# Attention and two mixtures on one core: the second mixture unit by unit over all chunks, the first with batch 0 alone ahead

## The chip, the cores and the metric

The kernel runs on 1 core of one Trainium2 chip. The metric is the device time of one execution in microseconds (us); below, the median of several runs.

## The reference

Three stages follow each other. `x` is 4 batches x 8 heads x 512 tokens x 64, `state` the same with 32 tokens.

```python
scores = scale * x @ state^T;  a = softmax(scores);   xread = a @ state
scores2 = scale * state @ x^T; a2 = softmax(scores2); sread = a2 @ x
t = concat([xread, sread], axis=2)            # -> 2176 rows x 512
# first mixture, 512 -> 2048 -> 512
h = t @ w_in;  t = (h * tanh(softplus(h))) @ w_out
# second mixture, 512 -> 1536 -> 512
xn = t / rms(t) * rms_g
g = xn @ w_gate; v = xn @ w_val; out = (g * sigmoid(g) * v) @ w_out2
```

## The kernel before

All matmuls of the mixtures take each float32 operand as a high and a low float16 part and make three products. A **chunk** is a batch's 512 xread rows (chunks 0 to 3); the 128 sread rows of all batches are the small chunk 4. A **unit** is 512 hidden columns: 4 units in the first mixture, 3 in the second.

*Order.* Nothing runs in the order of the source. Each `op(...)` records an instruction, its engines, a guessed cost and its dependencies; `Plan` (L36) list-schedules them by latest start times and then writes the instructions out, so every engine's queue has a fixed order. `at` is an op's place on TensorE, `P.floor` a time before which an op is not urgent. A queue that waits holds up all that stands behind it on that engine.

*Weights of the first mixture* (`plain`, L628) are fetched through the buffers `stage` in `psm` (a pool in SBUF), turned from the raw words to float32 and split into parts, on VectorE (DVE: L575, L582, L591, L625) and ScalarE (ACT: L472, L580, L612). `pow2` (L481) makes a power-of-two scale per unit from ACT's sums of squares: a tiny matmul (L485) and five small DVE instructions.

*First mixture* (`group`, `l2`). Groups 0 to 5 take units as they come: unit 0 for batch 0, then for batch 1, unit 1 for both, units 2 and 3 for both. Each group ends with four evacuations that add to what the group before left in a slot (L1053). Group 6 is batch 2, group 7 the small chunk, group 8 batch 3, each with all four units. Folds (L944) make the weights of the first product, L988 applies it, L1036 is the second product.

*Weights of the second mixture* (`seven`, `keep`): each of the nine matrices (gate, value and out for three units) is made into eight blocks (Strassen-like sums, L675) in one of two regions of `psm` and `attm` and stored to DRAM in `kept` tensors. All nine are made while the first mixture runs. `conv` is the last of these conversions.

*Second mixture* (`gated`). For chunk after chunk: `rms` of the next chunk (a chain of DVE and ACT instructions, L1072 to L1137), then for each unit `gate` and `value` (`quad`: 7 products of 12 matmuls each, L1174, and the adds L1186), and the first three products of the output (`first_three`, L1258). The PSUM banks `a0` to `a2` collect all three units of a chunk. `finish` then runs the other four products over three units each and combines the banks with five adds (L1288) and two copies (L472). SBUF holds the weights of two units at most, so the weights of units are loaded again for every chunk (`load`, L1452). The eighth block of each matrix lives in the slots of chunks that are done (`load_rest`, L1464, L1470).

Of the kernel before, what the change touches and what calls it, by code (L numbers as in the profile page):

```python
# [32 lines left out]
class Op:  # L33
    __slots__ = (
        "engs", "fn", "deps", "succ", "bufs", "tab", "at", "due", "reserve", "lat", "name", "floor")


class Plan:
# [10 lines left out]
    @staticmethod  # L49
    def hop(a, b):  # L50

        return 0.0 if a == b else 0.7 if b == "T" else 0.2 if a == "T" else 0.14
# [17 lines left out]
    def op(self, engs, fn, r=(), w=(), tab=None, at=None, reserve=0, lat=0.0, after=(), due=None, name=""):  # L70
# [3 lines left out]
        o.succ, o.bufs = [], []  # L74
# [106 lines left out]
    def forward(self, late):  # L181
# [18 lines left out]
        while True:  # L200
            moved = True
            while moved:
                moved = False
                for e in free:
# [3 lines left out]
                    for o in waiting[e]:  # L208
# [5 lines left out]
                        key = late[o] + pen, self.index[o]  # L214
# [105 lines left out]
def attn_moe_moe_kernel(  # L320
# [69 lines left out]
    sxm, xem = Mem("sxm", 4), Mem("xem", 2)  # L390
# [9 lines left out]
    for n, m in enumerate((w1, attm, w1)):  # L400
        home["wg", n], home["wv", n] = (m, 0), (m, 3584)

    def spot(w, u, j):

        if j == 7:
            k = ("wg", "wv", "w2").index(w) + 3 * u
            return slotm[k // 4], k % 4 * 512
        if w == "w2":
            return (psm, 1536 * u + 512 * j) if j < 3 else (attm, 2048 * u + 512 * (j - 3))
        m, at = home[w, u]  # L410
        return m, at + 512 * j

    slots_xe = [
        [(sxm, 0), (sxm, 512), (xem, 0)],
        [(w1, 7168), (w1, 7680), (w2m, 7168)],
    ]
# [6 lines left out]
    P.fifo.update(("t", "g", "g2", "gb", "xb", "xt", "t2", "t3", "sbt", "m", "m3"))  # L423
    P.pool("t", [tt(512 * k, 512) for k in range(10)])
    P.pool("g", [gm(512 * k, 512, F16).rearrange("p (l f) -> p l f", l=2) for k in range(6)])
    P.pool("g2", [w2m(512 * k, 512, F16).rearrange("p (l f) -> p l f", l=2) for k in range(14)])
    P.pool("gb", [psm(4608 + 512 * k, 512, F16).rearrange("p (l f) -> p l f", l=2) for k in range(3)])
    P.pool("m", [rmsm(512 * k, 512, F16).rearrange("p (l f) -> p l f", l=2) for k in range(4)])
    P.pool("m3", [m(at, 512, F16).rearrange("p (l f) -> p l f", l=2)
                  for m, at in ((psm, 4608), (psm, 5120), (psm, 5632), (slotm[3], 1280))])  # L430
# [50 lines left out]
    def pow2(part, pnames, k, floor, nm, xexp, most=0, to=None):  # L481
# [4 lines left out]
           r=pnames, w=[b], reserve=0, name=f"pow2 {nm}")  # L486
# [52 lines left out]
    def fetch(w, u, dst, dn, pool="raw", after=()):  # L539
# [10 lines left out]
        for v in range(2):  # L550
# [8 lines left out]
            for j in range(2):  # L559
# [6 lines left out]
                last = op({"A": a_sb(512), "V": v2(512)}, hi, r=[r], w=dn(k), after=after, name=f"hi {w}{u}{k}")  # L566
# [18 lines left out]
                for part, fn, engs in (("s", sign, "V"), ("l", low, "AV")):  # L585
                    cost = {e: a_sb(512) if e == "A" else v2(512) for e in engs}
# [344 lines left out]

    m_users = {"m": [], "m3": []}

    def fold(c, u, pool, after):

        out = []
        for g in range(2):
# [635 lines left out]
```

## Time and profile before

| | |
|---|---|
| median of 3 runs | 808.26 us (807.59 to 808.39) |
| the profiled execution | 810.53 us; its span from first to last instruction 808.7 us |
| TensorE (PE) busy | 725.2 us, 90% of the span, mean granted clock 0.939 |
| weight loads (PEld) | 505.7 us, 63% |
| VectorE (DVE) busy | 645.5 us, 80%, 1237 instructions |
| ScalarE (ACT) busy | 451.6 us, 56% |
| HBM | 101.45 MB read, 23.33 MB written |

The matmul's end is modelled, so PE's busy time is not work at full rate; how much work PE does must be counted from its instructions. PEclk of 1.00 is 2.4 GHz, 0.50 is 1.2 GHz; a mean between them is a mixture of both.

### The profile page before, as it was taken

To read this page: it belongs to the slowest core of one execution; us is meant where nothing else is said; L and a number is where in the kernel's file an instruction comes from. 1 tells how busy PE (TensorE), PEld (TensorE's weight loads), DVE (VectorE), ACT (ScalarE), POOL (GpSimd) and SP (SyncE) were. 2 spreads that over 40 slices of the span, in tenths; PEclk is the share of its full clock that TensorE was granted. 3 is DMA by queue.
4 is the path that set the end of the run, shared out by engine and by line. 5 is a ranking of instruction groups with operands and counts; after the bars stand their busy time and mean duration, and the time that the engine had idled before them with its cause. 6 is when DMAs were issued, how large, how long until landed. Compare 5 with 4: busy or idle time off the path is not lost.

```text
span 808.7 us, 13823 instructions
## 1 busy us (share of the span) xinstructions
PE 725.2 (90%) x5606; PEld 505.7 (63%) x5606; DVE 645.5 (80%) x1237; ACT 451.6 (56%) x804; POOL 1.6 (0%) x7
## 2 busy tenths in 40 slices
PE   4465799999997989589999999999996999999997
PEld 3243344445443336373476788888885889989996
DVE  6999999859999998999635699479996878465771
ACT  7998987826969889947531255135563332111320
POOL 0000000000000000000000000000000000000000
PEclk8655999999998999888999999999999899999999
DMA  8977101106156566571752324375457435364101
GB/s 266 303 205 228 53 1 66 53 1 209 53 183 200 191 220 224 206 277 74 279 188 108 117 64 171 102 270 202 138 194 281 145 105 183 105 265 158 61 2 66
DMA packets 40772, 125.68 MB, mean 155 GB/s; under 512 B 20484, under 2 KB 20484, under 8 KB 35716
## 3 DMA queue, kind: packets, MB, share of 16 engines
q1 hardware_dynamic: 40708, 124.79, 44.2%
q8 instruction: 44, 0.72, 0.3%
q14 instruction: 20, 0.16, 0.1%
HBM read 101.45 MB, written 23.33 MB: 154 GB/s over the span
## 4 chain that ended last, share of the span: by engine, by line
PE 42%; DVE 14%; ACT 1%; DMA 1%; issue 1%; DVEq 0%; SPq 0%; ACTq 0%
PE p L1174 21%; PE a L1258 10%; PE a L1036 5%; PE p L988 3%; PE p L1334 2%; DVE tt L1186 2%; DVE tt L1236 1%; DMA out_dram<-slot 1%; PE a L1372 1%; DVE slot L1101 1%; DVE tt L1225 1%; DVE w2m L1217 1%; DVE rms L1128 1%; DVE attm L625 1%; DVE psm L625 1%
## 5 line engine op out<-in xcount | busy, mean ns | idle before, releaser
L1036 PE MATMUL a<-g,w2m 128*128 128x512 f16 (+1 forms) x960 | 191.9, 356 | 9.3 <-DVE g L1014 9.1
L1036 PEld LDWEIGHTS <-w2m 128*128 128x128 f16 x960 | 88.6, 102 | 99.7 <-issue 17.9
L1174 PEld LDWEIGHTS <-w 128*128 128x128 f16 x1344 | 132.0, 98 | 25.4 <-issue 7.6
L1186 DVE TENSOR_TENSOR tt<-p,tt 128x512 f32<-128x512 f32 x120 | 82.3, 686 | 47.8 <-PE p L1174 46.8
L1174 PE MATMUL p<-slot,w 128*128 128x256 f16 x768 | 93.3, 273 | 3.6 <-ACT tt L472 3.6
L1174 PEld LDWEIGHTS <-attm 128*128 128x128 f16 x672 | 66.0, 98 | 12.8 <-DMA attm<-kept_wg 2.8
L988 PE MATMUL p<-slot,rms 128*128 128x512 f16 x288 | 70.6, 389 | 3.3 <-ACT tt L1010 3.0
L1258 PE MATMUL a<-attm,w2m 128*128 128x256 f16 x576 | 65.3, 273 | 0.0
L1258 PEld LDWEIGHTS <-w2m 128*128 128x128 f16 x576 | 56.3, 98 | 6.5
L988 PEld LDWEIGHTS <-rms 128*128 128x128 f16 x288 | 28.3, 100 | 40.7 <-issue 10.7
L1010 ACT ACTIVATE tt<-p,page 128x512 f32<-128x512 f32 x68 | 45.2, 678 | 14.9 <-PE p L988 13.1
L1258 PE MATMUL a<-psm,g 128*128 128x256 f16 x432 | 51.9, 273 | 0.0
L1014 DVE SCALAR_TENSOR_TENSOR g<-tt,page,g 128x512 f16<-128x512 f32 x68 | 49.6, 746 | 1.7 <-ACT g L472 0.5
L472 ACT ACTIVATE w2m<-tt 128x512 f16<-128x512 f32 x43 | 25.7, 621 | 41.5 <-DVE tt L1225 30.0
L1174 PE MATMUL p<-slot,attm 128*128 128x256 f16 x384 | 46.0, 273 | 2.6 <-DMA attm<-kept_wg 2.6
L1210 ACT ACTIVATE tt<-tt,page 128x512 f32<-128x512 f32 x36 | 25.9, 721 | 38.3 <-DVE tt L1186 38.1
L1258 PEld LDWEIGHTS <-g 128*128 128x128 f16 x432 | 42.2, 98 | 5.3 <-DVE g L1217 0.3
L472 ACT ACTIVATE g<-tt 128x512 f16<-128x512 f32 x24 | 14.1, 621 | 51.1 <-DVE tt L1236 42.9
L472 ACT ACTIVATE g<-tt,page 128x512 f16<-128x512 f32 x39 | 27.1, 712 | 26.5 <-PE a L1036 26.5
L472 ACT ACTIVATE psm<-psm,page 128x512 f16<-128x512 f32 (+1 forms) x42 | 29.8, 715 | 9.3 <-DVE psm L625 7.3
L287 ACT ACT_TABLE_LOAD x27 | 34.6, 1283 | 0.5
L944 PE MATMUL p<-w,slot 128*64 128x512 f16 x192 | 26.9, 401 | 7.9 <-ACT tt L1010 4.4
(222 smaller groups left out, 1198.1 us busy)
## 6 DMA issues: line engine op xcount, KB each, us to landing
w<-kept_wg SPq DMA_DIRECT2D x8, 1792.0 KB, 7.2
w<-kept_wv SPq DMA_DIRECT2D x8, 1792.0 KB, 7.3
attm<-kept_w SPq DMA_DIRECT2D x12, 1024.0 KB, 5.1
psm<-in_moe_w_out_dram SPq DMA_DIRECT2D x10, 1024.0 KB, 5.9
psm<-in_moe_w_in_dram SPq DMA_DIRECT2D x8, 1024.0 KB, 5.5
attm<-kept_wg SPq DMA_DIRECT2D x4, 1792.0 KB, 9.5
attm<-kept_wv SPq DMA_DIRECT2D x4, 1792.0 KB, 9.0
psm<-in_moe_w_gate_dram SPq DMA_DIRECT2D x6, 1024.0 KB, 5.2
```

What stands on the lines that cost most here:

```text
L287: self.nc.scalar.preload_act_table_set(TABLES[table])
L472: nc.scalar.activation(o, i, ACTF.Copy, scale=1.0 if scale is None else scale)
L625: op({"V": v1(512)}, lambda e: nc.vector.scalar_tensor_tensor(lo, f, s, h, ALU.mult, ALU.subtract), r=[*fn_, *hn, sname], w=ln, name=f"sl ...
L944: nc.tensor.matmul(P[pm][64 * j:64 * j + 64, :], states(c)[:, g, j, a, :], part("wi", u, 2 * g + j, b), start=(a, b) == (0, 0), stop=(a, b ...
L988: nc.tensor.matmul(P[ph], P[folds[u][k]][:, a, f:f + 128], xh[:, k, b, :], start=(k, a, b) == (0, 0, 0), stop=(k, a, b) == (1, 1, 0))
L1010: op({"A": a_ps(512) + 0.09}, lambda e, s=s, ph=ph, ce=ce: nc.scalar.activation(P[s], P[ph], ACTF.Mish, scale=ce), r=[ph, cen], w=[s], tab ...
L1014: op({"V": v1(512) + 0.06}, lambda e, s=s, g=g, rh=rh: nc.vector.scalar_tensor_tensor(P[g][:, 1, :], P[s], rh, P[g][:, 0, :], ALU.mult, AL ...
L1036: nc.tensor.matmul(P[ya[d]][:, :n], part("wo", u, f, a)[:, d * 128:(d + 1) * 128], P[g][:, b, i * n:(i + 1) * n], start=first and m == 0, ...
L1174: nc.tensor.matmul(P[to][:, f * 256:f * 256 + 256], part(w, u, j, a)[:, k * 256 + f * 128:k * 256 + f * 128 + 128], h[:, k, b, :], start=b ...
L1186: op({"V": v1(512) + 0.06}, lambda e: nc.vector.tensor_tensor(P[to], P[bank_], P[a], ALU.add), r=[bank_, a], w=[to], name=f"{w} add")
L1210: op({"A": a_ps(512) + 0.09}, lambda e, i=i, o=o: nc.scalar.activation(P[o], P[i], ACTF.Silu, scale=c3), r=[i, f"c3{u}"], w=[o], tab="silu ...
L1258: nc.tensor.matmul(P[to][:, t * 256:t * 256 + 256], P[g][:, a, o:o + 128], part("w2", u, j, b)[:, f * 256:f * 256 + 256], start=begin and ...
```

## The change

The second mixture's loops change places: unit outside, chunks 0 to 3 inside. Each weight block is loaded once (nine reloads of 1.8 MB; `follow` puts the next matrix where one has had its last use). `finish` now runs for each unit and chunk, 12 times and over one unit. For the first two units its results go to DRAM as partial sums (four stores of 256 KB in each finish, the small chunk one); in the last unit both partial sums are read back, added (`parts`) and joined to the result (`more`). All `rms` are recorded ahead of the loop, and their parts and the eighth blocks get places of their own (`places`). Scales are per unit (`gated_scale`).

In the first mixture group 0, 1 and 2 are batch 0 (unit 0, unit 1, units 2 and 3); batch 1, 2, 3 and the small chunk follow whole. Six conversions are recorded early, three with the second mixture (`late_keeps`). The small matmul of `pow2` is put ahead of all else as soon as it is ready (`brief`) but leaves one bank free. Guessed costs in the planner change a little. All matmuls stay.

```diff
-                        key = late[o] + pen, self.index[o]
+                        key = -1.0 if o.brief else late[o] + pen, self.index[o]
...
-           r=pnames, w=[b], reserve=0, name=f"pow2 {nm}")
+           r=pnames, w=[b], reserve=1, brief=True, name=f"pow2 {nm}")
...
-            lprod(to, gs[nm], u, j, u == 0)
+            lprod(to, gs[nm], u, j, True)
...
-    def finish(c, gss, oa, between=()):
+    def finish(c, u, gs, oa, between=()):
+        last = u == U2 - 1
...
+        home_ = "o" if (u, c) > (0, 1) else "t"
...
+        if last:
+            for v in range(U2 - 1):
+                at = 2048 + 2048 * v
+                op({"D": 2.95}, lambda e, at=at, v=v: nc.sync.dma_start(out=psm(at, 2048), in_=parts[v, c][:, :]),
+                   r=[("part", v, c, k) for k in range(4)], w=psm.names(at, 2048), lat=1.9, name="part")
+            for i in range(2):
+                for j in range(2):
+                    a, b = 2048 + 512 * (2 * i + j), 4096 + 512 * (2 * i + j)
+                    op({"V": v1(512)}, lambda e, a=a, b=b: nc.vector.tensor_tensor(
+                        psm(a, 512), psm(a, 512), psm(b, 512), ALU.add),
...
         def over(to, nm, j):
-            for u in range(U2):
-                lprod(to, gss[u][nm], u, j)
+            lprod(to, gs[nm], u, j)
...
+        def more(a, i, j):
+            if last:
+                v, n = q[i, j]
+                op({"V": v1(512)}, lambda e: nc.vector.tensor_tensor(two(P[a]), two(P[a]), v, ALU.add),
+                   r=n, w=[a], name="end more")
...
+        def put(o, i, j):
+            if not last:
+                k = 2 * i + j
+                op({"D": 0.74}, lambda e: nc.sync.dma_start(out=parts[u, c][:, 512 * k:512 * k + 512], in_=P[o]),
+                   r=[o], w=[("part", u, c, k)], lat=1.9, name="part")
...
     def gated():
         before = None
-        for c in range(B):
-            if c + 1 < B:
-                rms(c + 1, slots_xe[(c + 1) % 2])
-            for u in range(U2):
...
+        rms(2, slots_xe[2])
+        rms(3, slots_xe[3])
+        rms(B)
+        for u in range(U2):
+            at = B - 1 if u < U2 - 1 else B - 2
+            for c in range(B):
+                oa = [buf(("oa", u, c, k), f"a{k}") for k in range(3)]
                 ss = gate(c, u)
...
+                if before is not None:
+                    v, d, gs, ob = before
+                    first_three(v, gs, ob)
+                    finish(d, v, gs, ob)
+                    if d == B - 1:
+                        small_end(v, small)
+                        follow("w2", v)
+                gs = value(c, u, ss)
...
+    def follow(w, u):
+        k = units.index(w) + 3 * u
+        for n in range(k + 1, 3 * U2):
+            if home[units[n % 3], n // 3] == home[w, u]:
+                waiting_loads.append((units[n % 3], n // 3))
+                break
+        ready_loads()
...
         group(0, 0, [0], None, 2)
-        group(1, 1, [0], None, 3)
-        group(2, 0, [1], 2, 2)
-        group(3, 1, [1], 3, 3)
-        group(4, 0, [2, 3], 2, 0)
+        group(1, 0, [1], 2, 2)
+        group(2, 0, [2, 3], 2, 0)
...
-        group(5, 1, [2, 3], 3, 1)
+        group(3, 1, every, None, 1)
...
+        late_keeps = {(0, 2): ("wg", 2), (1, 0): ("wv", 2), (1, 1): ("w2", 2)}
```

In the built programs DVE has 1317 instructions for 1237, ACT three table loads more, and PE the same matmuls. The three places below are on VectorE, which feeds PE and is fed by it. `psm` and `attm` hold weights on their way, `rms` working tiles of `rms`, `tt` results of the products, `a_`, `p_` PSUM banks, `slot_` the chunks, `page_` scales.

The first is at the end of the first mixture, where the small chunk's group needs its low part `g` (L1014, L1010 in the changed kernel). Before:

```order
L476 TENSOR_SCALAR psm<-psm,page_68 128x512
L625 SCALAR_TENSOR_TENSOR psm<-psm,page_68 128x512
L476 TENSOR_SCALAR attm<-attm,page_68 128x512
L625 SCALAR_TENSOR_TENSOR attm<-attm,page_68 128x512
L1014 SCALAR_TENSOR_TENSOR g<-tt,page_117,g 128x512 x2
```

Of the change:

```order
L1087 SCALAR_TENSOR_TENSOR rms<-rms 128x512
L587 SCALAR_TENSOR_TENSOR psm<-psm,sxm 128x2x256
L1089 TENSOR_TENSOR rms<-rms 128x512
L1010 SCALAR_TENSOR_TENSOR g<-tt,page_114,g 128x512
L1091 SCALAR_TENSOR_TENSOR rms<-rms 128x512
```

Two matrices in work at once stood ahead of that group; now it is one matrix and the `rms` of batch 1, which came a whole chunk later before.

The second is in the middle of the second mixture, where the eighth blocks are split (L1470, L1538 in the changed kernel). Before, near the end of chunk 1:

```order
L1137 TENSOR_TENSOR w2m<-rms,w2m 128x2x256
L1288 SCALAR_TENSOR_TENSOR slot_77<-a_88,page_117,tt 128x2x256
L1083 TENSOR_SCALAR rms<-p_83 128x128
L1091 SCALAR_TENSOR_TENSOR rms<-rms 128x128
L476 TENSOR_SCALAR slot_77<-tt,page_68 128x512
L1470 SCALAR_TENSOR_TENSOR slot_77<-tt,page_68,slot_77 128x512 x3
```

Of the change, in its first unit:

```order
L1223 TENSOR_TENSOR tt<-tt 128x512
L1538 SCALAR_TENSOR_TENSOR w2m<-tt,page_68,w2m 128x512
L1173 TENSOR_TENSOR tt<-p_84,tt 128x512
L1204 TENSOR_TENSOR w2m<-tt,w2m 128x512
L1173 TENSOR_TENSOR tt<-p_85,tt 128x512
```

The blocks went into `slot_77`, whose result had just been made and had to be stored first, and `rms` of the small chunk stood beside them; now they go into `w2m` between products' adds.

The third is the end of the program. Before:

```order
L1217 TENSOR_TENSOR w2m<-tt,w2m 128x512 x2
L1288 SCALAR_TENSOR_TENSOR tt<-a_88,page_117,tt 128x512
L1288 SCALAR_TENSOR_TENSOR slot_79<-a_89,page_117,tt 128x2x256 x2
L476 TENSOR_SCALAR slot_80<-a_90,page_117 128x512
L1288 SCALAR_TENSOR_TENSOR slot_79<-a_88,page_117,tt 128x2x256
```

Of the change:

```order
L1304 TENSOR_TENSOR rms<-rms,psm 128x512
L1411 TENSOR_TENSOR tt<-tt 128x512
L1298 SCALAR_TENSOR_TENSOR rms<-a_89,page_114,rms 128x512
L1436 SCALAR_TENSOR_TENSOR slot_81<-a_91,page_114,tt 128x512
L1304 TENSOR_TENSOR rms<-rms,psm 128x512 x2
L1298 SCALAR_TENSOR_TENSOR slot_80<-a_90,page_114,rms 128x2x256
L1298 SCALAR_TENSOR_TENSOR slot_80<-a_89,page_114,rms 128x2x256
L1298 SCALAR_TENSOR_TENSOR slot_80<-a_88,page_114,psm 128x2x256
```

The adds of the last chunk's finish gain the joining of the partial sums (L1304, L1411) between them.

## Rows read from the trace of the kernel before

**Rows 1.** The page, part 1: busy us, share of the span, instructions.

```profile
PE 725.2 (90%) x5606; PEld 505.7 (63%) x5606; DVE 645.5 (80%) x1237; ACT 451.6 (56%) x804; POOL 1.6 (0%) x7
```

**Rows 2.** Stretches: length, busy PE, PEld, DVE, ACT, POOL; PE clock, DMA share, GB/s.

```profile
0.00:100.00 100.00, 56.62 (x367) 33.64 (x368) 89.54 (x223) 90.20 (x170) 1.60 (x7) 0.71 0.70 213
100.00:160.00 60.00, 59.04 (x288) 26.06 (x287) 57.60 (x125) 49.08 (x86) 0.00 (x0) 1.00 0.12 40
160.00:188.00 28.00, 28.00 (x206) 13.73 (x206) 16.93 (x37) 9.11 (x17) 0.00 (x0) 1.00 0.13 29
188.00:240.00 52.00, 51.30 (x318) 23.99 (x314) 49.81 (x103) 42.20 (x79) 0.00 (x0) 1.00 0.40 137
240.00:375.00 135.00, 110.66 (x767) 60.83 (x766) 125.67 (x253) 114.37 (x222) 0.00 (x0) 0.87 0.60 217
375.00:540.00 165.00, 164.97 (x1247) 121.04 (x1244) 111.91 (x183) 60.48 (x96) 0.00 (x0) 1.00 0.40 146
540.00:600.00 60.00, 59.09 (x530) 51.80 (x528) 58.14 (x94) 33.07 (x50) 0.00 (x0) 1.00 0.52 190
600.00:640.00 40.00, 32.84 (x275) 27.84 (x274) 29.90 (x59) 15.03 (x28) 0.00 (x0) 0.91 0.58 213
640.00:808.00 168.00, 162.68 (x1627) 146.75 (x1624) 105.95 (x166) 38.02 (x62) 0.00 (x0) 1.00 0.34 124
```

**Rows 3.** Chain that ended last: start us, us, engine, what.

```profile
376.63 3.88 PE a L1036 x18
...
447.00 14.41 PE p L1174 x132
...
777.41 10.48 PE a L1258 x96
...
799.68 3.94 PE a L1258 x36
803.65 0.75 DVE slot L1288
```

**Rows 4.** The same chain between 333 and 347 us.

```profile
343.75 0.75 DVE attm L625
344.50 1.32 DVE g L1014 x2
```

**Rows 5.** Who waited for whom, PE, 240 to 375 us: total, times, longest.

```profile
PE a L1036 <- DVE g L1014: 9.1, 2, 8.3
PE p L485 <- ACT junk L612: 4.2, 2, 2.1
```

**Rows 6.** The same, DVE, 100 to 200 us.

```profile
DVE g L476 <- PE a L1036: 7.0, 2, 5.1
DVE slot L1053 <- PE a L1036: 4.4, 4, 2.3
```

**Rows 7.** The same, all engines, 600 to 640 us.

```profile
ACT slot L472 <- DMA out_dram<-slot: 3.9, 1, 3.9
...
DVE slot L476 <- DMA out_dram<-slot: 3.6, 1, 3.6
...
PE p L1174 <- ACT tt L472: 2.9, 1, 2.9
...
PE p L1174 <- DMA attm<-kept_wg: 2.6, 1, 2.6
```

**Rows 8.** Groups of DVE instructions: busy us, mean ns | idle before.

```profile
L1186 DVE TENSOR_TENSOR tt<-p,tt 128x512 f32<-128x512 f32 x120 | 82.3, 686 | 47.8 <-PE p L1174 46.8
...
L1236 DVE TENSOR_TENSOR tt<-tt 128x512 f32<-128x512 f32 x48 | 32.4, 685 | 0.6
...
L1288 DVE SCALAR_TENSOR_TENSOR slot<-a,page,tt 128x512 f32<-128x512 f32 x12 | 9.0, 748 | 10.2 <-PE a L1258 10.1
```

**Rows 9.** DMA issues: count, KB each, median us to landing.

```profile
w<-kept_wg SPq DMA_DIRECT2D x8, 1792.0 KB, 7.2
...
tt<-kept_wg SPq DMA_DIRECT2D x3, 256.0 KB, 5.1
```

More of the change, by code (lines that the diff above doesn't have):

```diff
@@ L958, in fold, with group @@
         return out
[L960 removed]
+    def group(gi, c, us, before, after):
         n = width[c]
@@ L1301, in finish @@
+        if last:
+            c11, c12, c21, c22 = ((lambda v=v: v, n) for v, n in (place(0, 0), place(0, 1), place(1, 0), place(1, 1)))
+        else:
+            c11, c12, c21, c22 = ((t(o), [o]) for o in (x11, u2, a1, u3))
+        op({"A": a_ps(512) + 0.13, "V": v1(512) + 0.06}, lambda e: copy_to(e, two(P[a1]), two(P[A]), osc),
+           r=[A, on_], w=[a1], after=opened[1:] if home_ == "o" else (), name="end copy")
+        add(t(u2), [u2], B_, t(a1), [a1])
+        more(u2, 0, 1)
         over(B_, "S3", T3)
-        add(lambda: two(P[u3]), [u3], B_, a1)
+        add(t(u3), [u3], B_, t(a1), [a1])
@@ L1303, in finish @@
+        more(u3, 1, 1)
+        more(a1, 1, 0)
         over(A, "A12", W21)
-        scaled(lambda: c11[0], c11[1], A)
-        add(lambda: c22[0], c22[1], C, u3)
+        if last:
+            add(*c11, A, lambda: q[0, 0][0], q[0, 0][1])
+        else:
+            scaled(*c11, A)
+            put(x11, 0, 0)
+        add(*c22, C, t(u3), [u3])
+        put(u3, 1, 1)
         over(C, "S4", W22)
-        add(lambda: c12[0], c12[1], C, u2)
+        add(*c12, C, t(u2), [u2])
+        put(u2, 0, 1)
@@ L1310, in finish @@
         over(B_, "A22", T4)
-        add(lambda: c21[0], c21[1], B_, a1)
+        add(*c21, B_, t(a1), [a1])
+        put(a1, 1, 0)
+        if not last:
+            return
         for i in range(2) if c == B - 1 else [None]:
@@ L1426, in gated @@
-        finish(B - 1, *before, [lambda: small_end(small_gs)])
+                if c == B - 1 and u < U2 - 1:
+                    follow("wg", u)
+                if before is not None:
[6 more added lines that the diff above has]
+                gs = value(c, u, ss)
+                if c == at:
+                    small = small_value(u, sb_)
@@ L1429, in attn_moe_moe_kernel, with keep @@
+                if c == B - 1 and u < U2 - 1:
+                    follow("wv", u)
+                before = u, c, gs, oa
+                if (u, c) in late_keeps:
+                    later_keep(*late_keeps[u, c])
+                if c == B - 2 and u < U2 - 1 or c == 0 and u == U2 - 1:
+                    load_rest(u)
+        u, c, gs, ob = before
+        first_three(u, gs, ob)
+        finish(c, u, gs, ob, [lambda: small_end(u, small)])
     kept = {}
-    def keep(w, u, k, after):
+    def keep(w, u, k, floor, after=()):
```

298 lines of the change are left out of this document (145 added, 153 removed).

## The prediction

> **What bounds the kernel now.** I read the page's busy times first [rows 1]. PE is busy 90% of the span and DVE 80%. As PE's ends are modelled, I counted its work by matmuls instead. A 512-column matmul runs at 3.88/18 = 0.216 us and a 256-column one at 14.41/132 = 0.109 us, both at the full clock [rows 3]. All matmuls of the mixtures come to 647 us at these rates, and I estimate 38 us for attention, transposes and the small ones: 685 us of PE work. The change adds no matmul, so the span can only move by what stands beside these 685 us, which is 808.7 - 685 = 124 us.
>
> Where these lie shows in the stretches [rows 2]. I call the time less the PE work done until then PE's **lag**, counting the matmuls in each stretch at the rates above. The lag is 70 us at 100 us (fetching, conversion and attention, with the clock at 0.71), still 68 at 188, 105 at 375, 105 at 540, 107 at 600, 117 at 640 and 119 at the end; a tail of 5 us follows. So there are three places: the start, the stretch from 188 to 375 (37 us), and 540 to 660 (14 us).
>
> From 240 to 375 PE is busy 110.7 of 135 us at a mean clock of 0.87, while DVE is busy 125.7 of 135 [rows 2]: DVE is the bound there. The wait that ends last is on DVE's `g`, 9.1 us, 8.3 of it in one piece [rows 5], and in the chain that `g` stands right behind the splitting of weights in `attm` and `psm` [rows 4]. Just before, from 160 to 188, DVE was busy only 16.9 of 28 us and PE all of it [rows 2]; DVE waited 7.0 + 4.4 us for products [rows 6], having nothing else to do in its order. The late loss has another cause. From 600 to 640, ACT and DVE wait 3.9 and 3.6 us to write into a slot that is still being stored, PE then waits 2.9 us for a copy that stands behind this on ACT, and 2.6 us for a reloaded gate matrix [rows 7].
>
> **The change, part by part.** *DVE's work.* Counted in the built orders, five adds in each of 12 finishes instead of 4, one more in each of the last four, and the small chunk's, are 45 more scalar-tensor-tensor adds, at 748 ns [rows 8]. Joining the partial sums adds 29 plain adds at 685 ns [rows 8]. That is 33.7 + 19.9 = 53.5 us by rows, or 49 us as busy time (DVE's rows overlap: they sum to 703 us for 645.5 busy). Eight evacuations of the first mixture go, and 13 more copies are shared between ACT and DVE. Cover: from 375 us on DVE is busy 111.9 + 58.1 + 29.9 + 106.0 = 306 of 433 us [rows 2], so 127 us are idle; ACT has more. Without that cover the adds would cost 53.5 us.
>
> *The order.* What counts is how much DVE work stands ahead of a given matmul. For matmuls with the same PE work ahead of them, I summed the DVE instructions ahead of what they wait for, scaled to the page's busy time, and subtracted the PE work. This lead is the least lag that the order allows:
>
> | PE work ahead | 30 | 120 | 180 | 270 | 390 | 525 |
> |---|---|---|---|---|---|---|
> | lead before | 61 | 47 | 52 | 70 | 34 | 18 |
> | lead after | 59 | 54 | 55 | 47 | 59 | 29 |
>
> At 270 us of PE work 728 DVE instructions are needed before and 687 after. The hump at 270 goes, because batch 1 and batch 3 fill PE while the matrices are converted, and a lower one, from the `rms` of all chunks and the last conversions, comes at 390. (The three late conversions are not late in the built order: two end ahead of the second mixture's products, the third with its first chunks. The table has that in it.) Only this hump, 59 against 70, is a gain that the order guarantees.
>
> To the lead comes the time that DVE loses. Before, the lag at 375 us was 105 for a lead of 70: 35 us, which is DVE's idle time until then (375 - 339.6 busy) [rows 2]. After, I keep the 10 us of the first 100 us. Over the next 380 us, with DVE needed almost all the time, I bound the loss by the two nearest rows: 2.4 of 60 us (100 to 160), and 11.5 of 187 us (188 to 375) [rows 2], so 15 to 23 us. The 11 us of 160 to 188 need not come back, since the order leaves DVE no such lull (lead 54 and 55 for 47 and 52). The lag at 390 us of work is then 59 + 10 + 15 to 23 = 84 to 92; I take 88, in the middle, because each stretch mixes both kinds. Before it was 104.5 there. **Term 1: -16 us**; its ends are -27 (lag 77, where PE's own 70 is near) and -5.
>
> *The late loss.* The reloads for each chunk go (the gate's into `w` alone are 8 of 1.8 MB, 7.2 us each [rows 9]), no block is put into a slot being stored, and no `rms` stands there. DVE is fuller than before, as it was from 540 to 600: 58.1 of 60 us, while PE lost 0.9 us of idle time [rows 2]. Scaled to 265 us that makes 4 us for 14. **Term 2: -10 us**; ends -13 and 0.
>
> *Stores.* Each early finish stores four times 256 KB; a 256 KB load lands in 5.1 us [rows 9]. The four buffers in `rms` must be free at the next finish, 27.5 us of PE work later (two quads of 84 and one output of 84 matmuls at 0.109 us). I cost this at nothing; without the cover, at most 5 us for each of eight finishes, 40 us. The SP queue keeps its order, so a load that waits for a matrix's last use holds stores behind it; the only such places are the matrix changes, and no load stands there with less than a chunk to go.
>
> *The end.* In the last finish each product has 12 matmuls, 1.31 us, where 36 covered DVE's add for 3.94 us [rows 3]. Four adds of 0.75 us [rows 3] and three joins of 0.69 may show. From 0 to 5 us; I take the lower half, as the small chunk's product stands between. **Term 3: +2 us.**
>
> The sum is -16 - 10 + 2 = -24 us. The profiled execution took 810.53 us, 2.3 above the median of 808.26, so I expect 810.5 - 24 - 2.3 = **784 us**, with 776 to 796 where each term goes half-way to its ends.
>
> **The rivals.** *PE alone decides* (chance 0.11). If DVE stays ahead throughout, the lag stays near 72 in the plateau: -32, late -11, end +1, so 766 us. For it: from 100 to 188 PE lost nothing [rows 2]. Against: both engines are needed all the time, and each small wait of one is passed on.
>
> *The front keeps its losses* (0.16). DVE's losses move with it, waiting for raw weights, ACT's squares or banks; the wait for squares is 4.2 us from 240 to 375 [rows 5]. With 42 us of loss at 390 the lag is 101: -4, late -6, end +2: 800 us, up to no change.
>
> *Handoffs make it slower* (0.08). In each finish PE's next product on a bank waits for DVE to have read it. Before, three units stood between (3.94 us), now one (1.31 us). If one add of 0.75 us shows at each of 4 handoffs in 12 finishes, that is 36 us: 820 us. It decides from 24 us on, half a us for each handoff. For it: DVE will be busy about 355 of 410 us there. Against: from 540 to 600 DVE was 97% busy and PE lost 0.9 us [rows 2], and DVE's adds wait for PE 46.8 us in all [rows 8], seldom the reverse; the order puts other products' adds between a finish's adds. The Trainium skill (Perfetto Trace Analysis, Identifying the Most-Contended Engine) says that the engine with the highest occupancy is the one to relieve, and that for VectorE occupancy is a fair measure, while TensorE's headroom is to be read from its weight loads. By that rule DVE (80% against 63%) is the contended engine and loading it with 49 us more makes about 857 us. The trace does not bear it out for the second mixture: from 640 on DVE idles 62 of 168 us and PE is busy 162.7.
>
> *The clock* (0.04). Many short waits of PE could bring a mean clock of 0.91 to the second mixture, as from 600 to 640 [rows 2]: 9% of some 390 us, 35 us, 819 us. From 540 to 600, with short waits too, it stayed at 1.00. The Trainium skill (TensorE: Matmul & The Clock Gate, A second HAM failure mode: psum-queue depth-cycling) describes a kernel whose frequent micro-idles between groups made the clock swing between its levels; by it the shorter finishes speak for this rival.
>
> **How the numbers follow.** The forecast has 0.61. A measurement tells about 0.2%, 1.6 us. Faster are the forecast, PE alone, and most of the second rival (0.13): 0.85. No change is 0.04: the upper end of that rival (0.03) and 0.01 of the last two; the rest of those makes slower 0.11. The range is 766 to 803: below it lies half of the first rival, above it the last two and the upper part of the second.
>
> **What would show it.** Right: DVE busy near 694 us; from 240 to 375 us PE waits on DVE's `g` gone and the clock above 0.95; a lag near 88 where the second mixture's first unit ends; no wait on `out_dram` or on a reloaded matrix; PE without gaps over 1 us from there to the last finish. Wrong: DVE idle more than 30 us between 100 and 480, waits of PE on the end adds in every finish, or waits of DVE on stores of partial sums.

## The result and the profile after

The changed kernel takes **772.31 us** (median of 4 runs, 771.34 to 773.05); beside it on the same chip the kernel before takes 808.33 us. The ratio is 0.9555, with an interval of 0.9539 to 0.9572. The forecast was 784 us in a range of 766 to 803: sign and range held, and the gain is 12 us larger than forecast. The profiled execution took 771.34 us, its span 769.6 us (before 810.53 and 808.7 us).

The page's busy times, which answer to [rows 1]:

```profile
PE 705.1 (92%) x5606; PEld 494.4 (64%) x5606; DVE 683.2 (89%) x1317; ACT 454.2 (59%) x808; POOL 1.6 (0%) x7
```

DVE is busy 37.7 us more than before, and the span is 39.1 us shorter. The stretches that answer to [rows 2] (length, then busy time and count of PE, PEld, DVE, ACT, POOL; PE's clock, DMA share, GB/s):

```profile
0.00:100.00 100.00, 53.58 (x337) 29.07 (x338) 90.79 (x224) 92.19 (x167) 1.59 (x7) 0.73 0.70 213
100.00:160.00 60.00, 60.00 (x399) 28.33 (x398) 56.64 (x137) 56.40 (x102) 0.00 (x0) 1.00 0.22 67
160.00:188.00 28.00, 28.00 (x144) 12.60 (x144) 26.44 (x56) 24.00 (x38) 0.00 (x0) 1.00 0.26 95
188.00:240.00 52.00, 50.51 (x318) 23.15 (x314) 48.94 (x104) 40.71 (x81) 0.00 (x0) 1.00 0.48 172
240.00:375.00 135.00, 134.28 (x751) 64.84 (x750) 128.28 (x253) 101.61 (x198) 0.00 (x0) 1.00 0.53 189
375.00:540.00 165.00, 158.45 (x1560) 138.34 (x1559) 143.17 (x249) 78.75 (x129) 0.00 (x0) 1.00 0.24 85
540.00:600.00 60.00, 60.00 (x554) 53.80 (x553) 52.31 (x85) 18.67 (x30) 0.00 (x0) 1.00 0.25 85
600.00:640.00 40.00, 40.00 (x415) 36.39 (x413) 29.81 (x48) 12.32 (x19) 0.00 (x0) 1.00 0.45 159
```

From 240 to 375 us PE goes from 110.66 busy at a clock of 0.87 to 134.28 at 1.00, and from 600 to 640 us from 32.84 to 40.00. Of the waits of PE from 240 to 375 us [rows 5] only one is left:

```profile
PE p L1077 <- DVE rms L1072: 0.7, 1, 0.7
```

The lag, counted as in the prediction, answers to its terms:

| PE work done, us | 30 | 120 | 240 | 270 | 330 | 390 | 420 | 525 | 660 | tail after it |
|---|---|---|---|---|---|---|---|---|---|---|
| lag before | 70.5 | 67.6 | 85.1 | 104.8 | 103.6 | 104.4 | 104.6 | 117.3 | 118.7 | 5.4 |
| lag after | 67.7 | 67.8 | 62.7 | 62.8 | 68.8 | 73.7 | 75.1 | 75.2 | 75.1 | 9.9 |

**Term 1** (lag at 390) is -30.7 us, forecast -16. **Term 2** (from there to the end: 1.4 us instead of 14.3) is -12.9, forecast -10. **Term 3** (tail) is +4.5, forecast +2. The sum is -39.1 us, the difference of the spans. The 38 us of PE work for attention and the small matmuls are an estimate. So the entries up to 240 are rough: with these matmuls priced by their columns at one rate they move by up to 10 us, those of both kernels from 270 on by 2 at most. The fall of the lag between 120 and 240 lies within that.

### The profile page after: what moved, and what is told of

Read it like the earlier page. It is cut to its first block, busy times and chain, and to the rows that moved or that the text cites. A ratio compares the mean times of both kernels' runs of the same rounds, so it can differ in the third digit from the quotient of the medians.

```text
span 769.6 us, 13980 instructions
## 1 busy us (share of the span) xinstructions
PE 705.1 (92%) x5606; PEld 494.4 (64%) x5606; DVE 683.2 (89%) x1317; ACT 454.2 (59%) x808; POOL 1.6 (0%) x7
## 3 DMA queue, kind: packets, MB, share of 16 engines
HBM read 67.90 MB, written 32.24 MB: 130 GB/s over the span
## 4 chain that ended last, share of the span: by engine, by line
PE 47%; DVE 33%; ACT 12%; DMA 4%; issue 3%; SPq 0%; POOL 0%; POOLq 0%; ACTq 0%; DVEq 0%
PE p L1161 22%; PE a L1245 11%; PE a L1032 5%; PE p L984 4%; DVE psm L621 3%; DVE g L1010 3%; DVE tt L1173 2%; PE p L1372 2%; ACT sxm L576 2%; ACT junk L608 2%; DVE psm L472 2%; ACT w2m L468 2%; DVE attm L621 1%; ACT w L468 1%; DVE rms L1124 1%
## 5 line engine op out<-in xcount | busy, mean ns | idle before, releaser
L1161 PEld LDWEIGHTS <-attm 128*128 128x128 f16 x1008 | 98.4, 98 | 16.9 <-issue 5.6
L1161 PEld LDWEIGHTS <-w 128*128 128x128 f16 x1008 | 98.6, 98 | 11.3
L1173 DVE TENSOR_TENSOR tt<-p,tt 128x512 f32<-128x512 f32 x120 | 82.1, 684 | 21.6 <-PE p L1161 21.0
L984 PE MATMUL p<-slot,rms 128*128 128x512 f16 x384 | 90.8, 383 | 3.0 <-ACT tt L1006 3.0
L1161 PE MATMUL p<-slot,attm 128*128 128x256 f16 x576 | 69.7, 273 | 3.3 <-DVE tt L470 1.6
L1161 PE MATMUL p<-slot,w 128*128 128x256 f16 x576 | 69.3, 273 | 0.0
L1010 DVE SCALAR_TENSOR_TENSOR g<-tt,page,g 128x512 f16<-128x512 f32 x68 | 49.1, 744 | 0.6 <-ACT g L468 0.5
L1245 PE MATMUL a<-attm,w2m 128*128 128x256 f16 x384 | 46.7, 273 | 2.3 <-DVE rms L1298 1.3
L576 ACT ACTIVATE sxm<-psm 128x512 uint16<-128x512 uint16 x49 | 37.0, 779 | 10.7 <-DMA psm<-in_moe_w_out_dram 6.7
L621 DVE SCALAR_TENSOR_TENSOR psm<-psm,page 128x512 f16<-128x512 f32 x49 | 36.6, 746 | 1.5 <-ACT psm L468 0.8
L1298 DVE SCALAR_TENSOR_TENSOR rms<-a,page,rms 128x512 f32<-128x512 f32 x38 | 28.3, 745 | 7.7 <-PE a L1245 7.6
L1245 PE MATMUL a<-attm,g 128*128 128x256 f16 x288 | 34.7, 273 | 0.0
```

The lines of the kernel that those rows point to most:

```text
L576: nc.scalar.activation(s16[:, :, 0], r16[:, :, 1], ACTF.Copy, scale=2.0 ** -13, bias=2.0 ** -14 - 0.5)
L621: op({"V": v1(512) + 0.06}, lambda e: nc.vector.scalar_tensor_tensor(lo, f, s, h, ALU.mult, ALU.subtract), r=[*fn_, *hn, sname], w=ln, nam ...
L984: nc.tensor.matmul(P[ph], P[folds[u][k]][:, a, f:f + 128], xh[:, k, b, :], start=(k, a, b) == (0, 0, 0), stop=(k, a, b) == (1, 1, 0))
L1010: op({"V": v1(512) + 0.06}, lambda e, s=s, g=g, rh=rh: nc.vector.scalar_tensor_tensor(P[g][:, 1, :], P[s], rh, P[g][:, 0, :], ALU.mult, AL ...
L1161: nc.tensor.matmul(P[to][:, f * 256:f * 256 + 256], part(w, u, j, a)[:, k * 256 + f * 128:k * 256 + f * 128 + 128], h[:, k, b, :], start=b ...
L1173: op({"V": v1(512)}, lambda e: nc.vector.tensor_tensor(P[to], P[bank_], P[a], ALU.add), r=[bank_, a], w=[to], name=f"{w} add")
```

## Experiments

Each edit goes through the planner again, so the order of the whole program moves with it. The lag tells where a difference arose. All ratios are to the kernel before on the same chip.

### Which side of the change brings the plateau

The first four runs put one side of the change back or carry it over alone. Theory A gave term 1 to the first mixture (groups, powers, cost guesses), theory B to the second mixture's new order.

`b_groups`, the kernel before with the new groups:

```diff
-        attention(1)
...
+        attention(1)
...
-        group(1, 1, [0], None, 3)
-        group(2, 0, [1], 2, 2)
-        group(3, 1, [1], 3, 3)
-        group(4, 0, [2, 3], 2, 0)
+        group(1, 0, [1], 2, 2)
+        group(2, 0, [2, 3], 2, 0)
...
-        group(5, 1, [2, 3], 3, 1)
+        group(3, 1, every, None, 1)
```

> The kernel before, with the changed kernel's order of the first mixture alone (batch 0 alone on the first conversions, then batch 1, then batches 2 and 3; the second attention recorded after all plain tails). Theory A, the first mixture's order holds the 31 us that term 1 turned out to be worth: in its built order the DVE work needed ahead of PE's 270th us of work still leads by 65 us (70 before, 47 in the changed kernel), so by the lead alone 5 us go, but if the waits for conversions and powers go with the old order, 20 to 30 us go: 780 to 790 us, and the lag at 390 us of PE work is 75 to 85. Theory B, the gain sits in when the second mixture's matrices are converted against the first mixture's products: 800 to 808 us, lag at 390 about 100, with the wait of over 5 us on the gates g near 345 us still there.

Measured: 796.25 us, ratio 0.9835 (0.9819 to 0.9852), lag 92.2 at 390 us of PE work: between the theories.

`b_both` adds the powers:

```diff
-                        key = late[o] + pen, self.index[o]
+                        key = -1.0 if o.brief else late[o] + pen, self.index[o]
...
-           r=pnames, w=[b], reserve=0, name=f"pow2 {nm}")
+           r=pnames, w=[b], reserve=1, brief=True, name=f"pow2 {nm}")
```

> The kernel before, with the new order of the first mixture and the new handling of the powers (put first when ready, with one of the two spare accumulators' bank held back). Theory A: as the run with the groups alone or up to 5 us faster, 775 to 788 us, the PE gaps before the powers (8.6 us between 100 and 375 us in the kernel before) gone. Theory B: 800 to 808 us, lead 63 at 270 us of PE work and a lag there above 95.

Measured: 792.62 us, 0.9793 (0.9778 to 0.9809), lag 86.5: between again. Its stretch from 240 to 375 us:

```profile
240.00:375.00 135.00, 125.28 (x892) 67.28 (x891) 128.88 (x252) 107.56 (x205) 0.00 (x0) 0.99 0.53 194
```

PE gains 14.6 us of busy time there over [rows 2], with as much DVE work.

`a_groups`, the changed kernel with the old groups (the diff of `b_groups` backwards):

> The changed kernel with the old order of the first mixture (batches 0 and 1 in turn on the first conversions, the second attention early). Theory A: the plateau's gain is lost, 795 to 803 us, lag at 390 us of PE work about 100. Theory B: the second mixture's new order keeps it, 770 to 776 us; its lead is 39 to 50 between 240 and 390 us of PE work (47 to 59 in the changed kernel), so the lag stays at 68 to 76.

Measured: 773.81 us, 0.9559 (0.9544 to 0.9573), lag 71.7: theory B. In the changed kernel the order of the groups is worth nothing measurable.

`a_pow2`, the changed kernel with the old powers (`reserve=0`, no `brief`):

> The changed kernel with the powers as before (no bank held back, no priority). Theory A, with the powers as its part: gaps of PE before the powers come back, 5 to 10 us, 777 to 782 us. Theory B: 769 to 774 us. In its built order DVE has far less to do ahead of PE between 210 and 330 us of PE work (lead 20 to -2 against 46 to 53) and again 34 at 390; so if the lead, and not PE's own floor near 68 us, set the plateau, the lag would fall to 55 or less there and the time to 760 us or less. I expect the floor to hold: a lag does not fall unless PE's work stands idle behind nothing, and PE cannot make up time once lost.

Measured: 791.74 us, 0.9774 (0.9755 to 0.9794): slower than both allowed, and not by gaps before the powers. The lag was lower than in the changed kernel (57.1 at 240 us of PE work, below the 68 that I had taken for a floor; the entries are rough there) and then jumped from 61.0 to 88.1 between 330 and 345. PE's waits from 375 to 440 us:

```profile
PE p L1161 <- DMA attm<-kept_wg: 21.3, 1, 21.3
```

That is the reload of the second mixture's first gate matrix. SP's timeline (start, length, line) shows why it is late:

```profile
351.32 0.32 SPq L1500 DMA_DIRECT2D w<-kept_w  x1
393.42 0.32 SPq L1489 DMA_DIRECT2D kept_wv<-psm  x1
402.64 0.32 SPq L1489 DMA_DIRECT2D kept_wv<-psm  x1
403.05 0.38 SPq L1500 DMA_DIRECT2D attm<-kept_wg  x1
```

It stands in SP's queue behind stores of blocks that DVE had not split yet, and goes out at 403.05 us as soon as the last of them has gone; in the changed kernel it goes out at 311.6. Without priority, four of the second mixture's powers had been made by 312 us, where the changed kernel had made eight. So here, as far as this one run tells, the priority keeps the stores, and with them the queue, moving. It is no source of term 1: with other groups and guesses the old powers do no harm (`a_second`, below).

The next pair carries over the whole first mixture, or all but it. `b_first` is `b_both` with the new cost guesses too; `a_second` is the changed kernel with the old groups, the old powers and the old guesses (such as these):

```diff
-        return 0.09 if a == b and a in 'VA' else 0.0 if a == b else 0.7 if b == "T" else 0.2 if a == "T" else 0.14
+        return 0.0 if a == b else 0.7 if b == "T" else 0.2 if a == "T" else 0.14
...
-            op({"A": a_sb(size) + 0.07}, fn, r=ns, w=[q, (nm, "n", i)], lat=SLACK, name=f"sq {who}")
+            op({"A": a_sb(size) + 0.17}, fn, r=ns, w=[q, (nm, "n", i)], name=f"sq {who}")
```

> The kernel before with everything the change does to the first mixture: the order of the groups, the handling of the powers, and the planner's new cost guesses. The second mixture is the old one. Theory A, the first mixture's order holds term 1: 778 to 785 us, lag at 390 us of PE work 74 to 80, and only the late loss (14 us) left of the difference. Theory C, formed on the four runs before this one (the same 31 us are reached from either side, because what costs is DVE standing without work while a power of two is outstanding, and each part only shortens such a stop): the guesses give at most 5 us on top of the 792.6 us of groups and powers together: 787 to 793 us. Its built order leads by 68 us at 270 us of PE work, so a lag under 80 there would speak against lead plus idle time of DVE as the rule.

Measured: 791.94 us, 0.9798 (0.9783 to 0.9812): theory C, the guesses add nothing.

> The changed kernel with everything of the first mixture as before: old groups, old handling of the powers, old cost guesses. Only the second mixture's rearrangement is left. Theory A: 795 to 805 us, the plateau's gain lost and the late loss not. Theory B, the second mixture's conversions and order alone bring it: 770 to 778 us. Theory C: between, 780 to 795 us, with stops of DVE of 20 to 50 us in all between 100 and 375 us in front of outstanding powers, as in the run with the old powers alone (there about 60 us).

Measured: **770.81 us**, 0.9530 (0.9513 to 0.9546): theory B. The second mixture's rearrangement alone brings the whole gain; the first mixture's side brings 17 us to the kernel before (`b_first`) and nothing on top of the second mixture's. Theory C falls: DVE stood without work far longer here than in the changed kernel, and it cost nothing:

```profile
188.00:240.00 52.00, 51.84 (x321) 23.58 (x320) 34.24 (x80) 23.27 (x36) 0.00 (x0) 1.00 0.00 1
240.00:375.00 135.00, 132.29 (x779) 64.89 (x778) 117.61 (x213) 101.52 (x191) 0.00 (x0) 1.00 0.37 135
375.00:540.00 165.00, 156.53 (x1517) 136.32 (x1516) 161.35 (x292) 104.50 (x182) 0.00 (x0) 1.00 0.42 151
```

### Why: when the last matrices must be ready

What differs shows in the stretches of one line alone, the low part of a split (L625 before, L621 in the others), which every converted block passes. Busy time and count of DVE, then clock, DMA share and GB/s, of the kernel before:

```profile
240.00:375.00 135.00, 30.89 (x42) 0.87 0.60 217
375.00:440.00 65.00, 5.23 (x7) 1.00 0.41 154
440.00:640.00 200.00, 0.00 (x0) 0.98 0.47 170
```

and of `a_second`:

```profile
240.00:375.00 135.00, 19.43 (x26) 1.00 0.37 135
375.00:440.00 65.00, 6.66 (x9) 1.00 0.41 155
440.00:640.00 200.00, 20.46 (x28) 1.00 0.41 147
```

Before, chunk 0 goes through all three units at once, so all nine matrices had to be converted about when the second mixture begins: in its order 92 of 99 splits are needed at 270 us of PE work. With the unit outside, the last unit's matrices are needed 220 us of PE work after the first product (two units of four times 27.5 us) and not 55. In `a_second` 48 of 97 are needed at 270, and 28 splits run after 440 us.

The changed kernel makes far less use of this:

```profile
240.00:375.00 135.00, 27.15 (x37) 1.00 0.53 189
375.00:440.00 65.00, 5.20 (x7) 1.00 0.18 70
440.00:640.00 200.00, 0.00 (x0) 1.00 0.30 105
```

Its splits run at about the same times as before, 88 of 95 by 375 us in both; only PE is further on by then. Counted at 270 us of PE work (374.8 us before, 332.8 in the changed kernel, 330 in `a_second`), DVE has been busy for 339.5, 309.3 and 272.2 us. The five lines that convert weights (L575, L582, L591, L625, L675 and what answers to them) make up 165.6, 152.3 and 102.9 us of this. So in `a_second` nearly the whole difference is conversion put off. In the changed kernel conversion is 13.3 of 30.2 us; as much, 13.1 us, is `rms` of chunk 0, done by then before and not begun in the changed kernel, and 5.8 us are evacuations that went (other work is 2 us more). The rest of the 42 us of lag, 11.8 us, is less idle time of DVE.

Theory H: the later due time of the last matrices is what term 1 consists of. `a_deadline` puts the requirement back into the changed kernel and leaves the rest:

```diff
+        for n, (w, u) in enumerate((("wg", 2), ("wv", 2), ("w2", 2))):
+            last = keep(w, u, 0, T0 + KEEP0 + KSTEP * (6 + n), [bar])
+            if w == "w2":
+                gated_scale(u)
...
+        op({"X": 0.01}, lambda e: None, w=part_names("wi", 0, range(4)), after=last, name="conv all")
         group(8, 3, every, None, 3)
...
-        late_keeps = {(0, 2): ("wg", 2), (1, 0): ("wv", 2), (1, 1): ("w2", 2)}
+        late_keeps = {}
...
-KEEP0, KSTEP = 90, 25
+KEEP0, KSTEP = 60, 14
```

> The changed kernel with one requirement put back that the second mixture's old order made: all nine matrices of the second mixture must be converted before batch 3 of the first mixture begins (the conversions are released earlier for it, 14 us apart from 82 us on). The rest of the change stays. In its built order 96 of the splits are needed at 270 us of PE work (92 of 99 before, 82 of 97 in the changed kernel, 48 with only the second mixture changed), and the DVE work needed ahead leads by 78 us at 240 us of PE work. Theory H, the change's gain in the plateau is that the conversions of the last matrices may come later: the lag at 270 to 390 us of PE work is 78 plus DVE's idle time until then (15 to 25 us), so 93 to 103, and the time 790 to 800 us. Rival I, the gain comes from elsewhere in the second mixture's order (no reload between chunks, the x blocks and normalizations spread over the chunks): 772 to 778 us, lag below 80.

Measured: **814.63 us**, 1.0065 (1.0047 to 1.0083). That is far above rival I's range, and above H's too. The lag is 76.0 at 225 us of PE work, 112.7 at 240 and 118.0 at 390: the whole gain is gone. Its stretch from 240 to 375 us, and PE's longest wait from 100 to 440 us:

```profile
240.00:375.00 135.00, 95.57 (x430) 41.83 (x428) 108.22 (x213) 81.76 (x160) 0.00 (x0) 0.82 0.52 186
```

```profile
PE p L481 <- ACT junk L608: 35.0, 2, 17.8
```

The form differs from the kernel before: there PE waited for `g` behind the splits [rows 5], here two powers stand in PE's queue until ACT's squares of the late matrices come. These two waits, 35.0 us, are most of the 44 us of lag that the changed kernel does not have. The requirement is put as one hard wait, which can cost time whatever the gain came from. So this run shows that such a due time can cost the whole gain, not that the kernel before lost its time by it, and it does not refute rival I: `rms` of chunk 0 above is of rival I's kind. What is shown is the side of the change that brings term 1, the second mixture's rearrangement. That later conversions are the main part of it is borne out by the counts in `a_second`; in the changed kernel the shares of conversions, `rms` and evacuations are counted and not tested one by one.

### The late loss

`b_rest`, the kernel before with two reloads put later:

```diff
-                    if c + 1 >= B - 1:
-                        load_rest(c - B + 2)
+                if c == B - 1 and u == 0:
+                    load_rest(1)
...
+                    if c == B - 2:
+                        load_rest(0)
```

> The kernel before with the reload of the small chunk's gate parts and of the first stored activations put about a unit later in the order. It leaves the plateau as it is and tests the late loss (14 us between 540 and 660 us, of which 8.7 us are PE idle time after 600 us). Theory D, reloads that wait for a slot still being stored cause it: 3 to 8 us faster than before, 800 to 805 us. Rival E, the loss is DVE's own work in the third chunk's block and rms: no change, 807 to 810 us.

Measured: 801.17 us, 0.9907 (0.9892 to 0.9922): theory D. The lag grows by 5.7 us between 390 and 570 us of PE work, where it grew by 14.2 before, no engine waits on `out_dram` between 540 and 720 us, and the stretch is full:

```profile
600.00:640.00 40.00, 39.73 (x359) 34.90 (x358) 30.73 (x50) 15.45 (x26) 0.00 (x0) 1.00 0.59 217
```

So most of term 2 was the reloads into a slot still being stored [rows 7], and the kernel before could have had 7.5 us without the change.

### The end

`a_nojoin` reads back and joins nothing for chunks 0 to 3 (12 adds into the finishes go with the 16 joins, and 8 loads of 1 MB, not 32):

```diff
-            for v in range(U2 - 1):
+            for v in range(0):
...
-            if last:
+            if False:
```

> The changed kernel without reading back and joining the partial sums of the four large chunks in the last unit: the output lacks the first two units' share there. 16 plain adds of DVE (11 us) and their 32 loads go; the stores stay. Theory F (prediction's term 3, the joins are hidden but for the last): 766 to 770 us, 2 to 5 us saved, all of it after 735 us, the lag of 75 us until then unchanged. Rival G, stores and loads of partial sums collide with other transfers: more than 6 us saved, some of it before 735 us.

Measured: 765.18 us, 0.9471 (0.9444 to 0.9498). That is 7.1 us less than the changed kernel, more than F allowed. Theory F holds for the tail, 5.6 us instead of 9.9. Another 3.4 us are there by 330 us of PE work (65.2 for 68.8), some 400 us into the run, while the changed kernel stores its first partial sum at 437.5 us: another order, not transfers, though G's figure (more than 6 us) is met. The last stretch of the changed kernel and of this run:

```profile
735.00:769.60 34.60, 25.31 (x229) 22.14 (x227) 27.92 (x45) 5.46 (x9) 0.00 (x0) 0.94 0.44 164
```

```profile
735.00:762.00 27.00, 21.76 (x198) 19.11 (x196) 19.09 (x30) 4.82 (x8) 0.00 (x0) 0.99 0.27 99
```

`a_pool` gives the joins to GpSimd (the same edit for the small chunk's):

```diff
-                    op({"V": v1(512)}, lambda e, a=a, b=b: nc.vector.tensor_tensor(
+                    op({"G": 1.3}, lambda e, a=a, b=b: nc.gpsimd.tensor_tensor(
```

> The changed kernel with the 17 plain adds that join partial sums given to GpSimd. No row of the traces so far shows such an add on GpSimd. Theory J, DVE's adds bound the last 35 us (DVE busy 27.9 of 34.6 us): leaving all joins out saved 7 us, so if GpSimd's add takes under 2 us and does not slow DVE, 766 to 770 us. Rival K: GpSimd's add is slow (over 3 us) or slows DVE while it runs, and the last finish waits for its four: 772 to 785 us.

Measured: 772.41 us, 0.9554 (0.9527 to 0.9581), no gain. The group of GpSimd:

```profile
L1282 POOL TENSOR_TENSOR psm<-psm 128x512 f32<-128x512 f32 x16 | 23.8, 1514 | 728.5 <-DMA psm<-part 720.5 <-DVE tt L1223 8.0
```

1.51 us is under J's bound, but rival K's other condition holds: DVE slows while GpSimd adds. At 707 us four joins of GpSimd meet three of DVE's adds that read SBUF twice (L1223):

```profile
707.70 6.30 POOL L1282 TENSOR_TENSOR psm<-psm 128x512 f32<-128x512 f32 x4 [102.17 <-DMA psm<-part]
707.89 4.98 DVE L1223 TENSOR_TENSOR tt<-tt 128x512 f32<-128x512 f32 x3
712.79 0.68 DVE L1173 TENSOR_TENSOR tt<-p,tt 128x512 f32<-128x512 f32 x1
```

These three take 1.63 to 1.75 us each, in the changed kernel 0.68; the add that reads one input from PSUM (L1173) keeps its 0.68 us in the same stretch. GpSimd's own adds take 1.26 us at the least, and 1.71 between these. PE then waits 2.0 us for a finish (L1298) that stands behind them: from 700 to 735 us it is busy 32.96 of 35 us, in the changed kernel all 35. In the last finish the four joins take 5.84 us where DVE takes 2.6, and the finish waits for them. The Trainium skill (GPSIMD Engine Reference, Engine selection) says that GpSimd is about twice as slow as VectorE at adds of two inputs; the trace agrees, with 1.9 times (1.26 for 0.68 us) for its shortest adds.

### Using it

`a_later` converts the last unit's matrices a chunk or two later still:

```diff
-        late_keeps = {(0, 2): ("wg", 2), (1, 0): ("wv", 2), (1, 1): ("w2", 2)}
+        late_keeps = {(1, 0): ("wg", 2), (1, 1): ("wv", 2), (1, 2): ("w2", 2)}
```

> The changed kernel with the last unit's three matrices converted one or two chunks later still. Theory H: its built order leads by 35 to 46 us between 240 and 420 us of PE work, 10 to 18 less than the changed kernel; with DVE idle for 18 to 25 us until then that is a lag of 60 to 68, under or at PE's own 67.7 us, so the lag stays near 68 instead of rising to 75: 763 to 767 us. Rival: the later conversions take DVE's time from the adds of the second mixture's first unit or hold up a load, no gain: 770 to 776 us.

Measured: **767.96 us**, 0.9491 (0.9473 to 0.9510): faster than both kernels, the intervals of the ratios do not overlap. It lies just above theory H's 763 to 767 and below the rival's range: the lag at 390 is 69.1 instead of 73.7, but it did not stay near 68; the end lag is 72.5.

`a_best` goes further: the last chunk's partial sums are read into free space in `attm` too, the guesses are the old ones, `late_keeps` is that of `a_later`, and the conversions are released later:

```diff
+                n = 2048 if v == 0 else 1536
+                m = attm(3584 + 2048 * v, n)
...
-KEEP0, KSTEP = 90, 25
+KEEP0, KSTEP = 105, 25
```

> The changed kernel with four alterations that the runs before point to: conversions of the second mixture released 15 us later, the last unit's matrices recorded a chunk or two later, the planner's old cost guesses, and the last chunk's partial sums read into a place of their own, so that they can be joined before the last finish. In its built order the DVE work needed ahead leads by 51 us at 30 us of PE work (59 in the changed kernel), by 44 to 46 at 330 to 420 (53 to 59), and by -8 at 660 (4). Theory H with the rule that the lag is the larger of PE's own and the lead plus DVE's idle time: lag at 30 us of PE work 61 to 63, at 420 us 64 to 68 (lead 44, DVE idle 20 to 24 us), tail 6 to 8 us: 756 to 763 us. Rival: something that the lead does not see (squares on ACT, a reload in front of a product, as in the run with the old powers) takes the place: 766 to 775 us.

Measured: 771.80 us, 0.9547 (0.9531 to 0.9563): the rival. The lag starts as hoped (59.9 at 30 us of PE work), but is 71.0 at 330 and 75.4 at 420. PE's waits from 200 to 390 us:

```profile
PE p L481 <- ACT junk L608: 4.7, 4, 2.2
PE p L984 <- ACT tt L1006: 2.3, 2, 2.0
```

From the start to 390 us of PE work, the changed kernel, `a_later` and `a_best` in turn:

```profile
0.00:463.80 463.80, 409.55 (x2766) 228.76 (x2767) 438.05 (x921) 369.08 (x672) 1.59 (x7) 0.94 0.44 149
```

```profile
0.00:459.10 459.10, 409.13 (x2763) 231.03 (x2764) 423.08 (x882) 367.50 (x677) 1.60 (x7) 0.94 0.43 144
```

```profile
0.00:464.40 464.40, 418.10 (x2765) 231.03 (x2766) 433.15 (x888) 372.39 (x694) 1.59 (x7) 0.94 0.44 148
```

By that point DVE did 15.0 us less in `a_later` and was idle 36.0 us instead of 25.8: 4.7 us are left. In `a_best` it did only 4.9 us less, though the order asks for 7 to 15 less (leads of 44 to 46 for 53 to 59), and was idle 31.3 us: nothing is left. The lead is a bound for a lag, and what is taken from it comes back in part as idle time. Why the changed kernel, `a_groups`, `a_second`, `a_later` and `a_best` all end with a lag of 72 to 77 us, from 58 to 65 at 240, stays open: many small waits, none of them large.

## Why the prediction was right, and where it was off

**What bounds it** held: the gain came at the places named, from 188 to 375 us and from 540 to 660, and PE's 685 us, counted from the same matmuls, did not move. From 188 to 375 us the wait on `g` [rows 5] is gone and the clock is 1.00. The cause that I gave for the vanished hump, "batch 1 and batch 3 fill PE while the matrices are converted", failed as the cause: with the old groups the gain is as large (`a_groups`, `a_second`), though the new groups alone do take 12 us of lag from the kernel before (`b_groups`). In its place the runs put the second mixture's new order, by which conversions and `rms` come due later. The prediction's bracket, that the late conversions are not late in the built order, is right for the changed kernel (88 of 95 splits by 375 us, as before); and its lead at 270 (47 for 70) has the fall, 23 us where the trace shows 30, but for another reason.

**Term 1 was mis-sized**, -30.7 for -16, beyond its end of -27. The prediction put the lag at 390 at lead 59 + DVE's loss of 25 to 33. DVE's loss was 25.8 us (463.8 - 438.05), inside that. The lead was wrong: by then DVE had worked 438.05 us, 48 more than PE's 390, not 59 more. The 11 us are in the price of DVE's work, for which I scaled rows by one factor for the whole kernel: 694 us forecast, 683.2 measured. The rows of what DVE had done by 463.8 us sum to 498.4 us; at the prediction's factor (645.5/703) that is 458, against the 449 that its lead means, so the amount of work was about right. The kernel before could have told: its rows sum to 713.3 us, not 703, a factor of 0.905, but up to 375 us to 383.8 for 339.6 busy, 0.885; in the changed kernel it is 0.879 up to 463.8 us. The rows of the added work do sum to what was forecast (all of DVE's rows: 766.7 us for 713.3, 53.4 more for 53.5), but busy time rose by 37.7 instead of 49. Where the queue is full, rows overlap more, as the timeline of DVE in the last finish shows (start, length, then xcount):

```profile
745.52 1.88 DVE L1304 TENSOR_TENSOR rms<-rms,psm 128x512 f32<-128x512 f32 x3
754.83 1.89 DVE L1282 TENSOR_TENSOR psm<-psm 128x512 f32<-128x512 f32 x3
756.64 0.68 DVE L1304 TENSOR_TENSOR rms<-rms,psm 128x512 f32<-128x512 f32 x1
757.24 0.68 DVE L1411 TENSOR_TENSOR tt<-tt 128x512 f32<-128x512 f32 x1
757.84 0.74 DVE L1298 SCALAR_TENSOR_TENSOR rms<-a,page,rms 128x512 f32<-128x512 f32 x1
```

An add whose row lasts 0.68 us is followed by the next after 0.60. The measured terms (-30.7, -12.9, +4.5) lie nearer to those of the rival "PE alone decides" (-32, -11, +1; 766 us) than to the forecast's, and up to 375 us the trace shows what that rival says: PE is busy 272.8 of the 275 us from 100 on. Only from 375 to 540 us did PE lose 6.5 us, with DVE busy 143.17 of 165. The plateau of 88 that the forecast rests on was not there. The sign came from a mechanism that held in part; that the time fell into the range is partly luck, since the range reaches down to that rival's time.

**Term 2** held: -12.9 for -10, near its end of -13, with the cause that [rows 7] show (`b_rest`). **Stores** cost PE nothing, as taken; DMA issues that answer to [rows 9]:

```profile
psm<-part SPq DMA_DIRECT2D x8, 1024.0 KB, 4.8
part<-rms SPq DMA_DIRECT2D x24, 256.0 KB, 2.3
w<-kept_wg SPq DMA_DIRECT2D x2, 1792.0 KB, 7.5
```

A store lands in 2.3 us, and PE is full from 500 to 640 us, while finishes store. ACT waited once for a store of a partial sum, 12.7 us up to 538.6 us, and PE did not wait for ACT. **Term 3** was +4.5 in its 0 to 5; `a_nojoin` gives the tail 4.3 us back, so it is the joins that show. **Handoffs** did not make it slower: the groups that answer to [rows 8] still wait for PE; PE waits for an add of a finish (L1298) only twice, for 1.3 and 1.1 us, at the end.

```profile
L1173 DVE TENSOR_TENSOR tt<-p,tt 128x512 f32<-128x512 f32 x120 | 82.1, 684 | 21.6 <-PE p L1161 21.0
L1298 DVE SCALAR_TENSOR_TENSOR rms<-a,page,rms 128x512 f32<-128x512 f32 x38 | 28.3, 745 | 7.7 <-PE a L1245 7.6
```

Their waits fell from 46.8 to 21.0 us: DVE's slack shrank and was not used up. The rule of the Trainium skill on the most-contended engine (Perfetto Trace Analysis, Identifying the Most-Contended Engine), from which the prediction estimated 857 us, is not borne out here: DVE went from 80% to 89% and the kernel became faster. **The clock** stayed at 1.00 from 100 to 640 us.

## What to carry to other kernels

Ask of a loop order when its last operand must be ready, not only how often it is loaded: here the unit outside let conversions and normalization come due later, and that side of the change brought the whole plateau's gain, -30.7 us, more than the late loss with its reloads (-12.9). To price it, sum the other engine's work ahead of a matmul in the built order and add that engine's idle time; but price a full queue by the spacing of back-to-back instructions and not by their rows or a mean over the kernel, and treat a lead taken away as a bound, since part of it returns as idle time. Parts of a change that cure the same loss do not add: here one side alone gave 17 us, the other 38, and both together 36.

## What the runs showed of the hardware

DVE's 128x512 float32 adds start 0.60 us apart when nothing holds them, while each row says 0.68; the rows of the changed kernel overlap by 83.5 us in all (766.7 - 683.2, from the records of the trace), those of the kernel before by 67.9. The same add takes 1.26 us on GpSimd at the least. At 707 us in `a_pool`, beside GpSimd's adds, DVE's adds with both inputs in SBUF took 1.63 to 1.75 us and GpSimd's 1.71, while a DVE add with one input in PSUM stayed at 0.68. PE and DVE were busy 92% and 89% of one span, and with 32.24 instead of 23.33 MB written to HBM neither of them waited for a store of a partial sum.
